# The transposing loads of x, from the fifth on, are issued from ScalarE's queue

## The chip, the cores and the metric

The kernel runs on one core of one Trainium2 chip. Its time is the device time of one execution in microseconds (us). The runs compared are several executions of each kernel; one more execution of each was recorded by the hardware profiler, and the tables below come from that one.

The core has five engines that work side by side, each with its own in-order instruction stream: TensorE (PE in the profile; its weight loads are PEld), VectorE (DVE), ScalarE (ACT), GpSimd (POOL) and SyncE (SP), which here does nothing but issue DMAs. A DMA is issued by an instruction in an engine's stream and then carried out by the core's 16 DMA engines; a semaphore tells of its landing. In the profile "SPq" and "ACTq" are the instructions that an engine's sequencer handles by itself, DMA issues among them.

## The reference

One ConvNeXt-V2 block on an image of 512 x 512 pixels with 96 channels, in bfloat16:

```python
out = jnp.zeros_like(x)
for i in range(K):                       # K = 3: depthwise 3x3, taps dw
    for j in range(K):
        out = out + xp[:, i:i+H, j:j+W, :] * dw[i, j]
h = _layernorm(out, axis=-1)             # over the 96 channels
h = jnp.einsum('bhwc,ce->bhwe', h, w1)   # 96 -> 384
h = _gelu(h)
gx = jnp.sqrt((h * h).sum(axis=(1, 2), keepdims=True) + 1e-6)
nx = gx / (gx.mean(axis=-1, keepdims=True) + 1e-6)
h = grn_gamma * (h * nx) + grn_beta + h
h = jnp.einsum('bhwe,ec->bhwc', h, w2)   # 384 -> 96
return x + h
```

The sum of squares gx runs over all pixels, so the second matrix product can't begin before all blocks have passed the first.

## The kernel before

The image is cut into 128 blocks of four rows. The program has two stages. In the first, every block is loaded, convolved, normalised and put through the first product and the GELU, only to gather gx (and to keep some of the results). In the second, the hidden values are recomputed or read back, and the second product, the sum with x and the store follow. The change touches the first stage alone.

The first stage is written as a loop over slots s, and each slot holds a piece of work for several blocks at different depths of the pipeline. In the order in which slot s records them:

- `load_x(s + 4)` (L214, called at L785): a transposing DMA that brings block s + 4 of x, channels on partitions, into one of six places of the ring `xT`.
- `stage_read` (L606): one DMA that reads a normalised block back from DRAM, `ynT<-yn_dram`. It waits for the four writes of that block, made one slot earlier.
- `stage_write` (L601): four DMAs `yn_dram<-yn` that write the block which GpSimd normalised in the slot before.
- `stage_bcast` and `stage_rows` (L585, L567), each in one slot of four: four DMAs `rbc<-r_dram` and two DMAs `r_dram<-rt` that carry the row of 1/sqrt(variance) of a batch of four blocks through DRAM and spread it over the partitions.
- `store_next` (L706): a third of a finished block of GELU outputs, `g_dram<-g`, in most slots.
- On GpSimd: `stage_newton`, `stage_norm` (`yn<-y_bf,rbc`), the squares `ysq<-y_bf`, and `stage_rstd`.
- On TensorE, ScalarE and VectorE, interleaved by `mlp_units` (L658): the nine taps of the convolution of block s in three bursts, and the units of the first product of a block read two slots earlier. ScalarE runs ten activations in such a slot: units 0, 2, 3, 4, 6 and 7, the evacuation `y_bf` of the convolution, and units 8, 10 and 11. VectorE takes the statistics of the GELU outputs and one third of the evacuation (`CAST y_bf`), before which stands the turn of `stage_turn` (L561), once in four slots.

All the DMAs of this list are issued by SP, in this order; there are 128 blocks, and every engine's stream keeps the order of the program (`InOrder`, L24 to L40, fixes it, which is why most instructions carry L35 as their line). In the first slots, before the product has blocks to work on, ScalarE also makes the squares.

The framework gives each DMA that SP or ScalarE issues one of eight semaphores, in turn. A DMA that is given a semaphore waits until the DMA that held it before has landed. The turn runs over the DMAs of both engines, in the order of the framework's own schedule.

Of the kernel before, what the change touches and what calls it, by code (L numbers as in the profile page):

```python
# [56 lines left out]
def kernel(  # L57
# [125 lines left out]
    with ExitStack() as p1:  # L183
        pe, dve, act, pool, sp = (InOrder(tc, e) for e in (nc.tensor, nc.vector, nc.scalar, nc.gpsimd, nc.sync))
# [28 lines left out]

        def load_x(b):  # L214
            s0 = b % NXT * GR
            sp.dma_start_transpose(
                out=xt_all[:, :, s0:s0 + GR, :].rearrange("p k r w -> p k (r w)"),
                in_=bass.AP(x.tensor, x.offset + b * GR * W * C, [[4 * C, GR * W4], [1, 4 * C]]))

# [5 lines left out]
        for b in range(min(2, NBLK)):  # L225
            load_x(b)
        act.activation(out=warm[:], in_=warm[:], func=ACTF.Gelu_apprx_tanh)
        for b in range(2, min(4, NBLK)):
            load_x(b)
# [552 lines left out]
        for s in range(last_slot + 1):  # L782
            get = lambda kind: at.get((s, kind), [])
            if s + 4 < NBLK:
                load_x(s + 4)  # L785
# [53 lines left out]
            else:  # L839
                b = mlp[0]  # L840
# [163 lines left out]
```

## Time and profile before

| what | before |
| --- | --- |
| time, three runs | 1546.52 us median (1536.55 to 1554.59) |
| profiled execution | 1546.16 us, of which the recorded span is 1544.4 us |
| busy, of the span | PE 1428.2 us (92%), ACT 1372.3 (89%), POOL 1297.4 (84%), DVE 1096.2 (71%) |
| transposing loads | 128, all issued by SP, the first at 0.7 us, the last at 915.1 us |
| first stage, convolution | TensorE's matmuls on `xT` start at 7.9 us and go on to 950 us |
| second stage | from about 1040 us to the end, some 500 us; no load of this kind in it |
| DMA | 427.57 MB; SP's queue 319.76 MB, GpSimd's 103.43 MB, ScalarE's 0.15 MB |

Busy time does not count DMA issues: SP has no busy time at all, and what its stream does is seen in the timeline alone. A line of the timeline gives the start in us, the length in us, the engine, the line, the operation, output<-input and how many instructions were merged; in brackets the idle time of the engine before it and what ended it. In the view of a tile the three numbers behind a group are the shortest, the median and the longest duration in ns.

### The profile page before, as it was taken

The numbers are of one execution on the slowest core, as the hardware profiler recorded it, in microseconds if no ns is written. First come the engines' busy times: TensorE is split into PE (matmuls) and PEld (weight loads), VectorE is DVE, ScalarE is ACT, GpSimd is POOL, SyncE is SP. The second block draws the span as 40 slices with busy tenths as digits, with TensorE's granted clock in tenths as the row PEclk, the third lists the DMA queues.
The fourth block names the chain that finished last, engine by engine and source line by source line (L and its number), as shares of the span: only waits on it lengthen the run. The fifth ranks groups of instructions, "written<-read, shape, count | busy, mean of one in ns | idle before, by whom it ended". The sixth has DMA issues, their size and how long they took to land. (4 is left out here: it accounts for less than half of the span.)

```text
span 1544.4 us, 66344 instructions
## 1 busy us (share of the span) xinstructions
PE 1428.2 (92%) x29245; PEld 879.6 (57%) x29245; DVE 1096.2 (71%) x1997; ACT 1372.3 (89%) x1588; POOL 1297.4 (84%) x917
## 2 busy tenths in 40 slices
PE   7879989989999899999999989879999999998998
PEld 3435545545454454555455545447777767776776
DVE  4617868888887888888888888885555555554555
ACT  5759988979898898998898979999999999999997
POOL 2558897898789889988898889729999999999997
PEclk9989999999999999999999999999999999999999
DMA  8878999999999999999999997659999999999997
GB/s 148 178 171 204 238 203 240 237 238 225 241 233 237 232 234 239 257 225 247 234 243 235 241 233 214 194 178 358 396 365 379 418 412 414 412 412 405 409 415 281
DMA packets 349994, 427.57 MB, mean 277 GB/s; under 512 B 230122, under 2 KB 279882, under 8 KB 345226
## 3 DMA queue, kind: packets, MB, share of 16 engines
q1 hardware_dynamic: 333464, 319.76, 78.3%
q0 software_dynamic: 14880, 103.43, 16.8%
q8 instruction: 229, 3.75, 1.0%
q14 instruction: 59, 0.48, 0.1%
q10 hardware_dynamic: 1362, 0.15, 0.1%
HBM read 216.68 MB, written 156.22 MB: 241 GB/s over the span
## 5 line engine op out<-in xcount | busy, mean ns | idle before, releaser
L35 ACT ACTIVATE g<-PS 128x512 bf16<-128x512 f32 (+2 forms) x1062 | 731.7, 799 | 101.1 <-PE PS L35 47.2
L35 DVE BATCH_NORM_STATS2 bst<-g 128x6 f32<-128x512 bf16 x1110 | 680.1, 677 | 135.3 <-ACT g L35 133.9
L35 PE MATMUL PS<-ynT,w1p 128*128 128x512 bf16 x2181 | 612.3, 384 | 26.8 <-ACT g L35 7.9
L35 ACT ACTIVATE gr<-PS 128x1536 bf16<-128x1536 f32 x360 | 498.9, 1458 | 19.3 <-PE PS L35 15.0
L35 POOL TENSOR_TENSOR yn<-y_bf,rbc 128x1536 bf16<-128x1536 bf16 x126 | 389.8, 3096 | 146.9 <-DMA rbc<-r_dram 79.1
L35 DVE TENSOR_TENSOR o_sb<-PS,xb 128x384 bf16<-128x384 f32 x512 | 277.2, 556 | 228.0 <-PE PS L35 182.4
L35 PE MATMUL PS<-xT,Wd 32*32 32x512 bf16 (+2 forms) x15336 | 382.4, 367 | 58.7 <-DVE y_bf L35 35.8
L299 POOL TENSOR_TENSOR xb<-xr,B2c 128x1536 f32<-128x1536 bf16 x118 | 368.2, 3132 | 5.1 <-DVE o_sb L35 2.8
L35 PEld LDWEIGHTS <-Wd 32*32 32x32 bf16 x15336 | 180.8, 89 | 268.4 <-issue 220.6
L35 POOL TENSOR_TENSOR ysq<-y_bf 128x1536 bf16<-128x1536 bf16 x114 | 313.4, 2749 | 11.4 <-DVE y_bf L35 11.4
L35 PEld LDWEIGHTS <-w1p 128*128 128x128 bf16 x2181 | 172.2, 98 | 176.6 <-issue 91.6
L35 PEld LDWEIGHTS <-gr 128*128 128x128 bf16 x4296 | 212.2, 98 | 71.8 <-issue 15.4
L35 PE MATMUL PS<-W2s,gr 128*128 128x96 bf16 x4224 | 223.8, 206 | 10.3 <-DVE o_sb L35 9.9
L35 ACT ACTIVATE y_bf<-PS 128x1024 bf16<-128x1024 f32 (+1 forms) x135 | 139.9, 1041 | 37.2 <-PE PS L35 37.2
L35 PEld LDWEIGHTS <-g 128*128 128x128 bf16 x1704 | 104.9, 98 | 60.8 <-issue 28.0
L35 PE MATMUL PS<-w1p,ynT 128*128 128x256 bf16 (+2 forms) x822 | 125.2, 272 | 8.8 <-ACT xT L35 3.2
L35 PE MATMUL PS<-g 128*128 128x128 bf16 x1464 | 122.4, 220 | 1.3 <-DVE PS L35 1.3
L35 DVE CAST y_bf<-PS 128x512 bf16<-128x512 f32 x121 | 81.0, 670 | 36.9 <-PE PS L35 36.8
L35 PEld LDWEIGHTS <-gl 128*128 128x128 bf16 x1680 | 82.9, 98 | 24.9 <-issue 3.0
L35 PE MATMUL PS<-W2s,gl 128*128 128x96 bf16 x1680 | 89.7, 206 | 1.4 <-DVE o_sb L35 1.1
L35 PEld LDWEIGHTS <-ynT 128*128 128x128 bf16 x822 | 63.9, 97 | 31.2 <-issue 13.4
L254 POOL DMA_DIRECT2D xr<-in_x_dram x115 | 63.8, 555 | 14.2 <-POOL xb L299 14.2
(99 smaller groups left out, 566.6 us busy)
## 6 DMA issues: line engine op xcount, KB each, us to landing
g_dram<-g SPq DMA_DIRECT2D x105, 512.0 KB
gl<-g_dram POOLq DMA_DIRECT2D x35, 1536.0 KB, 11.2
yn_dram<-yn SPq DMA_DIRECT2D x512, 96.0 KB
ynT<-yn_dram SPq DMA_DIRECT2D x128, 384.0 KB
out_dram<-o_sb SPq DMA_DIRECT2D x127, 384.0 KB
xr<-in_x_dram POOLq DMA_DIRECT2D x123, 384.0 KB, 7.0
ynT<-yn_dram SPq DMA_DIRECT2D x85, 512.0 KB
rbc<-r_dram SPq DMA_DIRECT2D x124, 128.0 KB
```

The costliest lines, as they stand in the source:

```text
L35: r = f(*a, **k)
L254: pq.dma_start(out=xr[:], in_=x[0, r0:r0 + GR].rearrange("r w c -> (r w) c").rearrange("(p g) c -> p g c", g=PXP))
L299: pq.tensor_tensor(out=xb[:], in0=grp[q]["xr"][:], in1=bias[:, None, :].to_broadcast([128, PXP, C]), op=ALU.add)
```

## The change

The issue of the load goes to ScalarE's stream for blocks 4 to 127; blocks 0 to 3, which are loaded ahead of the loop, stay with SP. The call stays where it was: `load_x(s + 4)` is the first thing that slot s records. The descriptors, the places in the ring and the data are the same.

```diff
         def load_x(b):
             s0 = b % NXT * GR
-            sp.dma_start_transpose(
+            (sp if b < 4 else act).dma_start_transpose(
                 out=xt_all[:, :, s0:s0 + GR, :].rearrange("p k r w -> p k (r w)"),
                 in_=bass.AP(x.tensor, x.offset + b * GR * W * C, [[4 * C, GR * W4], [1, 4 * C]]))
```

In the built program the streams of PE and DVE are the same as before, instruction by instruction. ScalarE's stream gains 124 DMA issues, each ahead of the first activation of its slot; SP's loses them. The waits follow: since ScalarE's stream has by then passed activations that wait for the convolution of the slot before, its load needs no wait for TensorE any more, but it keeps a wait for the DMA that held its semaphore before. In the steady slots that is nearly always the first or the second of the four writes `yn_dram<-yn` of the same slot, which SP issues; in a few slots it is a read or ScalarE's own load of the slot before. The first load on ScalarE, block 4, also waits for the landings of blocks 2 and 3, which SP issues.

## The prediction

> **What bounds the kernel now.** I read the busy times by stage first, then the timeline of SP's stream, then ScalarE's. Nothing of this kind is issued after 915.1 us, so the stage to read is the steady part from 200 to 915 us:
>
> ```profile
> core 0: us, PE busy (x) PEld busy (x) DVE busy (x) ACT busy (x) POOL busy (x), PEclk, DMA share, GB/s
> 200.00:915.00 715.00, 661.10 (x15915) 361.71 (x15914) 596.01 (x1026) 627.78 (x931) 619.23 (x463) 0.98 1.02 236
> ```
>
> PE is busy 92%, ACT 88%, POOL 87%: no engine is full, and each is near it. SP is missing from this table. Its stream over two slots:
>
> ```profile
> 500.05 0.32 SPq L35 DMA_DIRECT2D ynT<-yn_dram  x1
> 500.50 3.13 SPq L35 DMA_DIRECT2D yn_dram<-yn  x4
> 503.68 1.18 SPq L35 DMA_DIRECT2D r_dram<-rt  x2
> 504.96 0.41 SPq L35 DMA_DIRECT2D g_dram<-g  x1
> 505.47 1.93 SPq L35 DMA_TRANSPOSE xT<-in_x_dram  x1
> 507.58 0.45 SPq L35 DMA_DIRECT2D ynT<-yn_dram  x1
> 508.09 2.77 SPq L35 DMA_DIRECT2D yn_dram<-yn  x4
> 510.90 2.45 SPq L35 DMA_DIRECT2D rbc<-r_dram  x4
> 513.44 0.37 SPq L35 DMA_DIRECT2D g_dram<-g  x1
> ```
>
> Each issue starts about 0.05 to 0.2 us after the one before has ended. Adding up the single records from 200 to 915 us, SP is issuing for 625 of 715 us (writes 263, loads of x 191, rbc 60, reads 44, stores 40, r_dram 26); 38 of the other 90 us stand between a load and the read behind it, which often waits for its writes to land. So SP waits for hardly anything of the engines: its stream is full. Loads follow each other every 7.63 us, 30.5 us for four. ScalarE shows what is undisturbed:
>
> ```profile
> 234.86 3.90 ACT L35 ACTIVATE g<-PS 128x1024 bf16<-128x1024 f32 x6 [0.25 <-PE PS L35]
> 238.59 1.08 ACT L35 ACTIVATE y_bf<-PS 128x1024 bf16<-128x1024 f32 x1
> 239.50 2.07 ACT L35 ACTIVATE g<-PS 128x1024 bf16<-128x1024 f32 x3
> 241.92 1.51 ACT L35 ACTIVATE g<-PS 128x1024 bf16<-128x1024 f32 x2 [0.35 <-ACT g L35]
> ```
>
> From 234.86 to 241.92 a slot takes 7.06 us with 0.35 us idle. The difference between 7.06 and 7.63 are longer gaps. They come through GpSimd, which waits for the broadcast that SP issues late in its slot; GpSimd's view of the normalisation says so (idle us, times):
>
> ```profile
>   DMA rbc<-r_dram: 42.0, 14
>   ACT g L35: 29.0, 9
> ```
>
> Late GpSimd makes the turn on VectorE late, then the cast of y_bf, then TensorE's next burst.
>
> **What SP gains.** Without the load, SP's slot is a read (0.47), four writes (2.82), the gaps (0.25) and, before the next read, the landing of the fourth write, which by the semaphore updates in the trace comes 3.0 us after its issue ends: 6.6 us, with broadcast, rows and store inside that landing. That is less than ScalarE's 7.06, so SP stops being the bound. Late next is ScalarE: 4 x 7.06 = 28.2 us for four slots, and 0.6 for the aggregates on VectorE (2.77 us about every eleventh block, of which some 1.6 reach ScalarE). Against 30.5 that is 1.7 us, and with the loads from 116 to 915 us there are 26 such groups: **-44 us**.
>
> The Trainium skill (DMA: Bandwidth & Descriptors, section "Issuing engines are not separate DMA queues") says that issuing from several engines saves only the sequencer's time, usually small beside the DMA. Here the row speaks against "small": 2.06 us of the 6.0 that a load takes from issue to landing, on a stream that is full. By the page the gain would be near nothing, and a sum by it 44 us higher than the one below.
>
> **What ScalarE pays: the issue.** On SP the issue took this long, in the first slots and in the steady ones:
>
> ```profile
> L35 SPq DMA_TRANSPOSE xT<-in_x_dram x8: 1350/1451/2276, 65.4 to 108.9; - x8
> L35 SPq DMA_TRANSPOSE xT<-in_x_dram x93: 1388/2064/3113, 205.4 to 908.7; - x93
> ```
>
> The longer ones mostly stand right behind a store of g (mean 2.11 us, 81 of 93). ScalarE's stream has no such store, but the stage and its traffic are those of the second row. I take 2.06 and keep 1.45 as the lower end. Its cover is ScalarE's lead: the sequencer hands over activations ahead of their execution. Where its record of the wait ahead of a slot's first activation is seen, it begins about 1.85 us (median; 1.7 to 2.2 for most) before that activation starts, while unit 8 still runs and 10 and 11 are handed over. An issue fits in there, and only the rest delays the slot: with the 93 measured durations against the leads of the 104 slots, 25 us in all at 2.06 (most slots +0.3), 3 us at 1.45. One slot in four I count in the loop below: **+19**.
>
> **What ScalarE pays: the wait.** Its load of slot s now waits, in most slots, for the second write of the same slot to land. TensorE's and VectorE's work of the slot is queued behind it through unit 0 and the evacuation. Today the first write begins 0.9 to 3.0 us after the slot's first activation (mean by place in the batch), and the second lands 5.2 us after that; it would have to land some 1.8 us ahead of it. So SP and GpSimd must come to stand about 9 us earlier against ScalarE than now, which ScalarE pays once, by waiting: **+9**. From then on a loop closes that was open: cast of y_bf ends 5.3 us into slot t; squares on GpSimd 2.75; rstd 1.55; newton 2.95; norm 3.1; two writes 1.4; landing 3.8; issue 2.06; handover 0.1: 23.0 us to the first activation of slot t+3, where 3 x 7.06 = 21.2 stand now. Newton and rstd come once in four slots, so 1.8 us for each of 26 groups: **+47** (+32 with an issue of 1.45; nothing, if SP and GpSimd find slack that I do not see, for in the other slots the same loop is 18.5). SP's own waits for loads that hold its semaphores are an issue and 3.9 us of landing, a slot or more earlier; I cost them at nothing, under SP's new slack of 0.5 us a slot.
>
> **The start.**
>
> ```profile
> 0.74 21.00 SPq L35 DMA_TRANSPOSE xT<-in_x_dram  x8
> 10.60 1.02 ACT L35 ACTIVATE y_bf<-PS 128x1024 bf16<-128x1024 f32 x1 [7.71 <-PE PS L35]
> ```
>
> Block 3 is issued until 8.1 us and lands 3.2 later, at 11.3; only then may ScalarE issue block 4 (1.5 to 2), and the evacuation at 10.60 is behind it: **+3**. In the other early slots ScalarE idles 1.4 to 2.8 us ahead of an evacuation, which hides the issue; each load is needed three slots later, so a late one costs nothing.
>
> The skill (same page, section "Silent corruption: two transposing streams in flight at once") asks that the later stream's first transpose wait for the earlier stream's landing. This is that wait. No run here shows what happens without it; by the page it is due, and by the row it costs 3 us once.
>
> **Sum.** -44 + 19 + 9 + 47 + 3 = +34 us on the profiled execution's own 1546.16 us (span 1544.4 and 1.8 around it), which is 0.4 us under the median of the runs: **1580 us**, +2.2%. The second stage, from 1040 us, is untouched.
>
> **The rivals.**
>
> - *SP's freed stream wins* (faster). If SP and GpSimd run a slot ahead by themselves, the wait is over when ScalarE comes to it, and the issue takes 1.45: -44 + 3 + 3 = -38, **1508**. For it: SP's new slot of 6.6 us is shorter than 7.06, and SP alone holds the rate today. Against: GpSimd has 27 to 28 us of work in four slots of 28.2, so it can hardly draw ahead. It decides when the second write lands earlier than 1.85 us before the first activation of its slot.
> - *A draw.* The issue takes 1.45, the loop stays: -44 + 3 + 9 + 32 + 3 = +3, **1549**.
> - *The issue is not covered.* If the semaphore comes late in nearly every slot, the lead is lost and every issue stands whole between two slots: 104 x 2.06 = 214 on top of the 59 us of the start, the shift and the loop, less the 44: at most **1775**; with half of it, about 1665. For it: landings spread by over 1 us (3.0 to 4.6 for the second write), and every spread now hits ScalarE. It decides when the write lands later than 2.06 us before the first activation is due, in slots without newton too.
>
> That the loads stay with SP after all is excluded: they stand in ScalarE's stream of the built program.
>
> **How the numbers follow.** The forecast's case (1562 to 1630) gets 0.43, SP's gain 0.22, the draw 0.17, the uncovered issue 0.18. With the lower edge at 1512, a little above the rival's 1508, and the upper at 1665 about 2 in 10 are left out, half on either side. About 1% (15 us) is what a measurement of this kernel can tell from no change. Faster by more: 0.23; within: 0.17; slower: 0.60.
>
> **What would show it.** Right: SP's stream with gaps in the steady part; the second write of a slot landing close to the time ScalarE's sequencer reaches the load; ScalarE's gaps at slot starts grown to 0.6 us, and to 2 us or so in the newton slots; GpSimd's 42 us for rbc smaller. Wrong: issues on ScalarE of 1.4 us and gaps of 0.3, at 7.06 us a slot (SP's gain), or gaps of 2 us in every slot (no cover). Wrong as well, if issues on both queues slow each other down, which no row of this trace shows, as no two issues of its steady part run side by side on SP and ScalarE.

## The result, and the profile after

| what | before | after |
| --- | --- | --- |
| time, median of four runs each | 1546.43 us (1536.55 to 1554.59) | 1657.83 us (1640.01 to 1682.66) |
| profiled execution | 1546.16 us, span 1544.4 | 1640.01 us, span 1638.2 |
| last load of x is issued at | 915.1 us | 1008.6 us |
| from there to the end | 629.3 us | 629.6 us |
| mean from load to load, block 20 to block 127 (107 slots) | 7.61 us | 8.44 us |

The ratio of the times is 1.0639, with a 95% interval of 1.0521 to 1.0757 (two slower executions of the changed kernel, 1666.20 and 1682.66 us, at a lower clock, are left out of it though not of the median, so that 1546.43 x 1.0639 = 1645 us is the time to compare). The change made the kernel slower. The second stage is as long as before; at the start 4.8 us are lost up to the load of block 20 (105.7 us against 100.9); the rest, 107 x 0.83 = 89 us, is lost in the steady part of the first stage.

The busy times by stage of the changed kernel, for the same window as before:

```profile
core 0: us, PE busy (x) PEld busy (x) DVE busy (x) ACT busy (x) POOL busy (x), PEclk, DMA share, GB/s
200.00:915.00 715.00, 611.44 (x14253) 326.07 (x14253) 528.47 (x910) 559.01 (x828) 554.54 (x418) 0.96 0.92 211
```

Every engine does 8 to 11% less work in the same 715 us, and the DMA engines move 211 GB/s instead of 236: no engine has become the bound. The timeline of SP's stream:

```profile
506.31 1.17 SPq L35 DMA_DIRECT2D r_dram<-rt  x2
507.59 0.52 SPq L35 DMA_DIRECT2D g_dram<-g  x1
508.30 0.31 SPq L35 DMA_DIRECT2D ynT<-yn_dram  x1
508.67 3.32 SPq L35 DMA_DIRECT2D yn_dram<-yn  x4
512.03 2.63 SPq L35 DMA_DIRECT2D rbc<-r_dram  x4
514.76 0.37 SPq L35 DMA_DIRECT2D g_dram<-g  x1
515.30 0.40 SPq L35 DMA_DIRECT2D ynT<-yn_dram  x1
515.75 4.04 SPq L35 DMA_DIRECT2D yn_dram<-yn  x4
519.89 0.53 SPq L35 DMA_DIRECT2D g_dram<-g  x1
530.90 0.31 SPq L35 DMA_DIRECT2D ynT<-yn_dram  x1
```

SP has gaps now. From 200 to 1000 us it issues for 416 of 800 us, and 184 us of the rest stand between a store and the read behind it (mean 2.2 us). What SP waits for, by the view of its own waits in the 715 us (us in total, times, longest):

```profile
SPq L35 <- DMA yn_dram<-yn: 178.5, 101, 10.2
SPq L35 <- DVE y_bf L35: 61.3, 20, 7.0
SPq L35 <- DMA ynT<-yn_dram: 34.7, 23, 4.2
```

The first row was, before,

```profile
SPq L35 <- DMA yn_dram<-yn: 23.3, 36, 2.4
```

so SP now stands waiting for its own writes to land. ScalarE's timeline beside it:

```profile
506.60 1.53 ACTq L35 DMA_TRANSPOSE xT<-in_x_dram  x1
506.96 1.17 ACT L35 ACTIVATE g<-PS 128x512 bf16<-128x512 f32 x2
508.56 3.90 ACT L35 ACTIVATE g<-PS 128x1024 bf16<-128x1024 f32 x6 [0.43 <-PE PS L35]
512.29 1.09 ACT L35 ACTIVATE y_bf<-PS 128x1024 bf16<-128x1024 f32 x1
513.20 1.59 ACT L35 ACTIVATE g<-PS 128x1024 bf16<-128x1024 f32 x2
514.42 2.66 ACTq L35 DMA_TRANSPOSE xT<-in_x_dram  x1
514.58 0.70 ACT L35 ACTIVATE g<-PS 128x512 bf16<-128x512 f32 x1
517.20 3.90 ACT L35 ACTIVATE g<-PS 128x1024 bf16<-128x1024 f32 x6 [1.93 <-PE PS L35]
520.93 1.08 ACT L35 ACTIVATE y_bf<-PS 128x1024 bf16<-128x1024 f32 x1
521.84 2.08 ACT L35 ACTIVATE g<-PS 128x1024 bf16<-128x1024 f32 x3
530.23 1.32 ACTq L35 DMA_TRANSPOSE xT<-in_x_dram  x1
531.75 3.79 ACT L35 ACTIVATE g<-PS 128x1024 bf16<-128x1024 f32 x5 [7.84 <-PE PS L35]
```

At 506.60 the load is issued while activations run, and the slot opens with 0.43 us idle. At 514.42 the issue ends at 517.08 and the slot opens right behind it, after 1.93 us idle. At 530.23 the issue begins right behind the landing of a write (530.21 us), 6.3 us after the last activation has ended, and everything behind it has waited too. The gap ahead of a slot's first activation is 1.67 us in the mean over the 95 loads from 200 us on, against 0.80 before. That difference, 0.87 us, is about the whole loss of a slot (0.83). In 64 of the 95, the first activation starts within 0.25 us of the end of the load's issue. The 95 gaps are 158 us in all. In 42 of these us the load has not been issued yet, 92 lie under its issue, and 25 come after it. This tells where ScalarE idles and not yet why: the issue also hides other delays that end under it.

Why the write was so late at 530 is seen in the landings, which the semaphore updates in the trace give. The load, both stores, the read and the four writes issued from 514 to 520 us all landed 11 to 12.6 us after their issue; that is the worst stretch. From 200 to 900 us, from the end of the issue to the landing in us (10th percentile, median, 90th):

| DMA | before | after |
| --- | --- | --- |
| writes `yn_dram<-yn` | 2.32, 3.61, 4.62 | 2.96, 4.63, 7.29 |
| load of x | 2.69, 3.92, 4.30 | 3.04, 4.91, 7.69 |
| read `ynT<-yn_dram` | 3.78, 4.44, 5.20 | 3.45, 5.50, 8.06 |
| store `g_dram<-g` | 3.04, 3.98, 4.86 | 3.18, 4.48, 7.92 |

All four land later, by 0.5 to 1.1 us in the median and by 2.7 to 3.4 at the 90th percentile. For the writes it matters whether a load of x is in flight, that is, issued and not landed when the write's issue ends. From 200 us to the last load, with none in flight, the median and the 90th percentile are 2.86 and 3.72 us before (78 writes) and 2.53 and 3.73 after (37). With one in flight they are 3.74 and 4.69 before (296) and 4.73 and 7.24 after (343). The DMA engines' own work has not grown: the part of the page on DMA queues shows (packets, MB, share of 16 engines), before and then after,

```profile
q1 hardware_dynamic: 333464, 319.76, 78.3%
q10 hardware_dynamic: 1362, 0.15, 0.1%
```

```profile
q1 hardware_dynamic: 139032, 270.98, 52.1%
q10 hardware_dynamic: 195794, 48.93, 21.3%
```

That is 78.4% of 1544.4 us and 73.4% of 1638.2, or 1211 us and 1202. The packets take the same time in the sum, and still the DMAs land later.

### The profile page after: what moved, and what is told of

Read it like the earlier page. It is cut to its first block, busy times and chain, and to the rows that moved or that the text cites. A ratio compares the mean times of both kernels' runs of the same rounds, so it can differ in the third digit from the quotient of the medians.

```text
span 1638.2 us, 66328 instructions
## 1 busy us (share of the span) xinstructions
PE 1458.0 (89%) x29245; PEld 885.6 (54%) x29245; DVE 1095.7 (67%) x1997; ACT 1374.3 (84%) x1588; POOL 1299.0 (79%) x917
## 5 line engine op out<-in xcount | busy, mean ns | idle before, releaser
L35 PE MATMUL PS<-ynT,w1p 128*128 128x512 bf16 x2181 | 627.8, 387 | 93.4 <-ACT g L35 69.0
L35 PE MATMUL PS<-xT,Wd 32*32 32x512 bf16 (+2 forms) x15336 | 390.3, 373 | 49.0 <-issue 32.8
L35 PE MATMUL PS<-g 128*128 128x128 bf16 x1464 | 126.5, 224 | 1.3 <-DVE PS L35 1.3
```

Source lines behind the costliest of these rows:

```text
L35: r = f(*a, **k)
```

## The experiments

The changed kernel gave three candidates. **Wait**: ScalarE's load waits for SP's write of the same slot, and so closes the loop that the prediction feared. (Of the 95 loads, 51 wait for the second write of their slot, 18 for the first and 14 for the third, the others for other DMAs.) **Issue**: the time in which ScalarE's sequencer issues the load isn't covered. **Queues**: loads and the other DMAs are in flight on two queues, and all land late. Under the last it was open whether it takes full DMA engines, any second queue, or a transposing load on one of the two. Us per slot means the mean from the load of block 20 to the last, in the one profiled execution. Ratios are of several executions against the kernel before, with their 95% interval.

**1. The semaphores dealt anew** (changed kernel). Each DMA that SP issues first in a slot is listed behind ScalarE's load, so that the load takes its semaphore from a DMA of an earlier slot. Nothing else changes in the streams.

```diff
...
             if hasattr(r, "ins"):
                 self._tc.keep_in_program_order(r)
+                if name == "dma_start" and self._eng is self._tc.nc.sync and LAST_X:
+                    self._tc.add_manual_dep(r.ins, LAST_X.pop(), ...)   # order in the list, no semaphore
...
-            (sp if b < 4 else act).dma_start_transpose(
+            r = (sp if b < 4 else act).dma_start_transpose(
...
+            if b >= 4:
+                LAST_X[:] = [r.ins.name]
```

> Every engine's stream is that of the changed kernel, instruction by instruction; only the framework's list is told that SP's first DMA of a slot stands behind ScalarE's load of that slot. So the eight semaphores are dealt differently: the load of slot s waits for a DMA of slot s-1 or s-2 and no longer for a write of slot s. Theory 'wait' (ScalarE stalls because its load waits for the landing of a write that SP issues in the same slot): the waits ahead of the load, 120 us in sum from 200 us on, mostly go, and with SP's stream freed the time falls to the old kernel's or below, 1500 to 1550 us. Theory 'queues' (loads and other DMAs from two queues in flight at once slow each other's landing, whatever ScalarE waits for): the median landing of a write stays at 4.6 us and the time stays over 1600 us. Theory 'issue' (ScalarE can't cover the issue itself): 1570 to 1600 us, with gaps of 1 us or more at most slot starts and no wait ahead of the load.

Measured: 1622.91 us, 1.0456 (1.0406 to 1.0505), 8.35 us per slot (the profiled execution is the slowest of the four, 1638.48 us). ScalarE idled 6 us ahead of its issues instead of 42, and 58 us under them instead of 92, but the writes landed as late as in the changed kernel (2.75, 4.69, 6.64). (The expectation counts the sequencer's own wait, part of which passes while activations still run.) With most of the wait gone, 1.8 of the 6.4% come back; the two intervals leave room for 0.5 to 3.1. The late landings stay.

**2. A small DMA on ScalarE** (kernel before, x on SP). ScalarE issues a copy of 1.7 KB at the place where the changed kernel has the load.

```diff
+        tinyt = consts.tile([9, C], bf16, name="tinyt")
...
             if s + 4 < NBLK:
+                act.dma_start(out=tinyt[:], in_=dw.rearrange("kh kw c -> (kh kw) c"))
                 load_x(s + 4)
```

> The loads of x are all back on SP; ScalarE issues in their place, once in each slot, a load of 1.7 KB into a scratch tile that nothing reads (0.6 us of issue in the trace of the old kernel). It takes a semaphore in the turn, and waits for one, a write of the slot before. Theory 'wait': within 1% of the old kernel, 1535 to 1565 us, since the wait is a slot older than in the changed kernel. Theory 'queues': the same, for next to nothing is moved by the second queue. Theory 'issue': 0.6 us fits under the lead of 1.85 us, 1546 us as well. If it is over 1575 us, a DMA on ScalarE costs something that none of the three has.

Measured: 1559.88 us, 1.0056 (1.0033 to 1.0079), 7.65 us per slot. The view of its tile (shortest, median, longest in ns) shows the issue:

```profile
L35 ACTq DMA_DIRECT2D tinyt<-in_dw_dram x93: 278/279/302, 203.3 to 913.9; - x93
```

A wait and a short issue on ScalarE cost 0.04 us per slot in the profiled execution, the fastest of eight, and 0.6% by the ratio, while the writes land as before (3.60 in the median). All three candidates had expected this, so it parts none of them; it shows that a DMA on ScalarE as such costs little.

**3. The writes ahead of the read** (changed kernel). SP's writes no longer stand behind a read that waits for landings, so that they leave and land earlier for ScalarE.

```diff
-            for b in get("read"):
-                stage_read(b)
             for b in get("write"):
                 stage_write(b)
+            for b in get("read"):
+                stage_read(b)
```

> The changed kernel with SP's writes of a slot recorded ahead of its read, so that the writes no longer stand behind a read that waits for the landing of the writes of the slot before (184 us between a store and the read behind it, from 200 to 1000 us). The load still waits for a write of its own slot. Theory 'wait': the writes are issued 2 to 4 us earlier against ScalarE, and the waits ahead of the load fall by half or more: 1540 to 1590 us. Theory 'queues': the landing stays long, and the time stays within 2% of the changed kernel's, 1620 to 1680 us. Theory 'issue': the same, 1620 to 1680.

Measured: 1651.18 us, 1.0653 (1.0615 to 1.0691), 8.43 us per slot: no gain. The median landing of a write fell to 4.04 us and ScalarE's idle time ahead of the issues to 29 us, but the late landings stayed (90th percentile 7.09).

**4. The four writes as one DMA** (kernel before). To learn what SP's full stream is worth.

```diff
-            for r in range(GR):
-                sp.dma_start(out=yn_dst(b, r), in_=yn[32 * r:32 * r + 32, :, :])
+            t = yn_dram[b]
+            sp.dma_start(out=bass.AP(t.tensor, t.offset, [[W, GR], [NI * GR * W, 32], [GR * W, NI], [1, W]]),
+                         in_=yn[:])
```

> The old kernel (loads on SP), with the four writes of a block issued as one DMA of the same 384 KB. It measures the other reading of the old kernel by itself: if SP's full stream bounds the steady part (625 of 715 us issuing), and one issue of 384 KB costs about half of the four (2.8 us), SP gains some 1.4 us a slot and the steady part falls from 7.63 to 7.1 us a slot, 1490 to 1510 us in all. If SP's stream isn't the bound, 1535 to 1555 us.

Measured: 1825.68 us, 1.1779 (1.1725 to 1.1833), 9.60 us per slot. The writes' issue fell from 263 to 40 us of the 715, yet SP was issuing for 641 us, because its other issues grew: the load of x, 2064 ns in the median before, now

```profile
L35 SPq DMA_TRANSPOSE xT<-in_x_dram x75: 1754/3656/6582, 203.3 to 914.5; - x75
```

So the length of an issue on SP is not fixed: it grew beside a slower DMA of the same stream. The time of this kernel says nothing of a shorter stream, since the single DMA itself landed 8.4 us after its issue in the median. The next run repeats the question with another layout.

**5. The four writes as one DMA of 128 x 3 KB** (kernel before). The DRAM copy keeps the tile's order; the reads gather 1 KB runs instead.

```diff
-    yn_dram = dram.tile([NBLK, C, GR * W], bf16, name="yn_dram")
+    yn_dram = dram.tile([NBLK, GR * C, W], bf16, name="yn_dram")
...
     def yn_src(q):
-        return yn_dram[q].rearrange("c (r w) -> c r w", r=GR)
+        return yn_dram[q].rearrange("(r c i) w -> (c i) r w", r=GR, i=NI)
...
-            for r in range(GR):
-                sp.dma_start(out=yn_dst(b, r), in_=yn[32 * r:32 * r + 32, :, :])
+            sp.dma_start(out=yn_dram[b].rearrange("(p i) w -> p i w", i=NI), in_=yn[:])
...                                               # the second stage's reads take yn_src as well
```

> The kernel before (x on SP), with the four writes of yn as one DMA of 128 x 3 KB into a DRAM layout that keeps the tile's order, and the read gathering four 1 KB runs for each channel instead of one of 4 KB. SP has three issues fewer in each slot; bytes and the sum of 1 KB and larger packets stay. Theory SP (its stream of issues is the bound, the reading of the prediction): the writes' 2.8 us of issue a slot become about 0.7, SP's slot 5.5 us, so slots of 7.06 to 7.2 us, ratio 0.965 to 0.975. Theory DMA (the 16 engines are full, packets in flight for 709 of 715 us, and long issues are back-pressure): the loop does not get shorter, ratio 0.99 to 1.01, and the other issues on SP take longer than before.

Measured: 1588.19 us, 1.0253 (1.0214 to 1.0292). Of the 46 us that its profiled span is longer, 33 lie in the second stage, where the reads are in 1 KB runs; in the first stage a slot takes 7.71 us against 7.61. The window and what SP waited for in it:

```profile
200.00:915.00 715.00, 654.75 (x15943) 359.56 (x15915) 589.46 (x1015) 624.38 (x925) 618.70 (x463) 0.98 0.95 235
```

```profile
SPq L35 <- PE PS L35: 399.4, 93, 8.0
```

SP issues for only 375 of the 700 us from 200 to 900, and waits most of the rest for TensorE to leave the place in the ring. (The view counts into the issues. By the records, 286 us without an issue stand ahead of loads, and 91 of the 93 loads start right behind an update of TensorE's semaphore.) An SP with half its time free brings no shorter slot. One thing speaks against taking this as the whole answer: other DMAs landed later in this run, the write at 5.02 us and the broadcast at 5.10 in the median, where it was 3.60 and 2.84. So theory SP, on which the prediction's largest gain rested, is not borne out: freeing the stream is not enough. What a free SP with unchanged landings would bring is not shown.

**6 and 7. Ordinary copies in place of the transposing loads, on SP and on ScalarE.** The same bytes in 384 packets of 1 KB instead of 1536 of 256 B. The transposition is left out, so the convolution works on channels in the wrong places. The two differ only in the queue, and the second has the same waits ahead of the load as the changed kernel.

```diff
-            sp.dma_start_transpose(
-                out=xt_all[:, :, s0:s0 + GR, :].rearrange("p k r w -> p k (r w)"),
-                in_=bass.AP(x.tensor, x.offset + b * GR * W * C, [[4 * C, GR * W4], [1, 4 * C]]))
+            ...                                   # b < 4: as before
+                sp.dma_start(                     # 7: act.dma_start
+                    out=xt_all[:, :, s0:s0 + GR, :],
+                    in_=bass.AP(x.tensor, x.offset + b * GR * W * C, [[12 * 128, 128], [512, NI], [128, GR], [1, W4]]))
```

> The kernel before, with the loads of x from the fifth on as ordinary copies of the same number of bytes (384 packets of 1 KB in place of 1536 of 256 B): no transposition, so the channels are wrong and the output with them. Theory DMA: a load takes about 1.3 us of all engines instead of 2.7 (the price of 384 1 KB packets of the writes), the share of DMA falls from 1.02 to about 0.85, and the slots go to ScalarE's 7.06 to 7.2 us: ratio 0.965 to 0.975. Theory SP: the issue of a load falls to that of a write (0.7 us) and the ratio is the same, but then issues of the other DMAs keep their lengths (writes 0.7 us); by theory DMA they get shorter too. If neither bounds, 0.99 to 1.01.

> The changed kernel with the same ordinary copies in place of the transposing loads, on ScalarE's queue (output wrong in the same way). Against the same copies on SP. If a second queue as such makes all landings late, or ScalarE's wait for SP's writes: 3 to 6% slower than the copies on SP, landing of a write 4.5 us. If it takes full DMA engines, or the 1536 small packets of the transposing load mixed with others: within 1% of the copies on SP, landing of a write near 3.6 us or under it.

Measured, on SP: 1521.54 us, 0.9823 (0.9771 to 0.9875), 7.34 us per slot. On ScalarE: 1543.24 us, 0.9959 (0.9935 to 0.9982), 7.57 us per slot. The windows, on SP and on ScalarE:

```profile
200.00:915.00 715.00, 679.66 (x16633) 375.56 (x16631) 614.68 (x1064) 649.55 (x965) 643.69 (x482) 0.99 0.81 245
```

```profile
200.00:915.00 715.00, 664.21 (x16168) 365.31 (x16145) 598.24 (x1035) 631.65 (x940) 627.29 (x475) 1.00 0.79 240
```

Landing of a write: 2.54, 3.73, 4.98 on SP; 1.86, 3.66, 5.17 on ScalarE. The move costs 0.22 us per slot here, 1.4% (1543.24 / 1521.54), where it costs 0.83 with transposing loads, and the writes land no later. The other DMAs do, but less than in the changed kernel: load, read and store by 0.4 to 0.7 us in the median (0.5 to 1.1 there), and by at most 0.8 at the 90th percentile (2.7 to 3.4 there). Neither the second queue as such nor the wait and loop bring the writes' late landings or the long tails. But two things differ from the changed kernel: the load itself (no transposition, a quarter of the packets) and the DMA share, 0.8 for 0.9. The base speaks only half for full DMA engines: with a fifth of their time freed it gained 0.27 us per slot, not the 0.4 to 0.5 expected. ScalarE's issue is also shorter here, 547 ns; 25 us of idle time lie under the issues, and 21 ahead of them.

**8. The stores on ScalarE's queue** (kernel before, x on SP): another second queue, with 128 packets of 4 KB in most slots.

```diff
-                sp.dma_start(out=g_dram[whole.index(b)][:, h * n:h * n + n],
+                act.dma_start(out=g_dram[whole.index(b)][:, h * n:h * n + n],
```

> The kernel before (x on SP), with the stores g_dram<-g of the first stage issued on ScalarE's queue at their old place in the program's order. A second queue with 128 packets of 4 KB at a time. If a second queue as such lets packets of two DMAs mix and all land late: landing of a write from 3.6 to 4 us or more, ratio 1.02 to 1.06. If only the mixing of the transposing loads does it: landing of a write 3.6 us or under, ratio 0.99 to 1.01 (ScalarE's own issue was worth 0.6% in the run with a small DMA). Theory SP: its stream is relieved of 40 us of issues, ratio 0.97 to 0.99.

Measured: 1568.68 us, 1.0129 (1.0065 to 1.0192), 7.64 us per slot in the profiled execution, the fastest of the four. Landing of a write 2.28, 3.83, 4.94: a little later. This lies between the two sides: a second queue costs something even with transposing loads left on SP, but not 6%. SP's stream, relieved of the stores, brings no gain here either.

**9 and 10. Both kernels with quartered stores.** They take away DMA load and leave the transposing loads as they are. A quarter of each store of g is made, and the second stage reads it four times; the hidden values of the stored blocks are wrong in both.

```diff
...                                               # g_dram smaller; the second stage reads it four times
+                m = 512
-                sp.dma_start(out=g_dram[whole.index(b)][:, h * n:h * n + n],
-                             in_=flat(b)[:, h * n:h * n + n])
+                sp.dma_start(out=g_dram[whole.index(b)][:, h * m:h * m + m],
+                             in_=flat(b)[:, h * n:h * n + m])
```

> The kernel before (x on SP) with a quarter of each store g_dram<-g of the first stage: 128 x 1 KB in place of 128 x 4 KB. The second stage reads that quarter four times over, so bytes read there stay and the output is wrong for the stored blocks. It is the base of the next run; a store's three quarters are some 1.5 us of all 16 DMA engines, at 0.78 stores a slot. If the DMA engines' time bounds the old loop, its loads come every 7.1 to 7.3 us instead of 7.61 (mean from the 20th load to the last), ratio 0.965 to 0.98; if not, 7.5 to 7.65 and 0.99 to 1.0.

> The changed kernel with the same quartered stores. To be set against the run before it, as 8.44 us a slot of the changed kernel stands against 7.61 (+0.83). Theory full engines (two queues hurt because the engines have no slack, and small loads are drained alongside the writes): with slack the difference falls to +0.3 or less, 2% of the time, landing of a write near 3.7 us. Theory transposition (a transposing load beside ordinary DMAs of another queue is slow by itself, whatever the load): the difference stays +0.6 to +0.85 us a slot, 4.5 to 6.5%, landing of a write 4.3 us or more. ScalarE's wait for the write is there in both (one write later in the turn for many slots, as the scheduler deals the semaphores anew).

Measured: 1532.89 us, 0.9888 (0.9859 to 0.9916), 7.45 us per slot with x on SP; 1631.46 us, 1.0523 (1.0464 to 1.0582), 8.38 us per slot with x on ScalarE. The windows, in that order:

```profile
200.00:915.00 715.00, 670.47 (x16266) 369.87 (x16265) 607.82 (x1048) 639.27 (x951) 631.88 (x479) 0.98 0.85 193
```

```profile
200.00:915.00 715.00, 627.35 (x14722) 338.84 (x14723) 544.86 (x939) 577.17 (x854) 574.55 (x425) 0.96 0.82 175
```

The base's 7.45 us lies between its two sides again. The move costs 0.92 us per slot, 6.4% (1631.46 / 1532.89), no less than with full stores, at a DMA share close to that of runs 6 and 7. The writes land at 1.91, 3.22, 4.23 us with x on SP and at 2.73, 4.30, 7.37 with x on ScalarE. So the late landings don't need DMA engines as full as in the kernel before. In these runs they come when the transposing loads, with their 1536 packets, go out on another queue than the writes and reads.

**11. The writes ahead of the read in the kernel before**, the edit of run 3; a try at a faster kernel.

> The kernel before with the four writes recorded ahead of the read in each slot. A version to beat both: the writes leave SP 0.5 us earlier and the read that waits for its block's writes stands behind new issues, so the 38 us of SP's gaps between a load and a read go. Theory SP (its stream is the bound): 38 us over the loop, ratio 0.975 to 0.98. Theory DMA engines: 0.99 to 1.01.

Measured: 1603.69 us, 1.0346 (1.0316 to 1.0376), 8.02 us per slot, against both theories. The writes land sooner (median 3.08), but the broadcast, now right behind the read, lands at 4.20 us instead of 2.84, the load's issue grows to 2.58 us in the mean, and GpSimd's wait for the broadcast from 42.0 to 61.0 us. The order in SP's one queue is worth 3% by itself. No run here is a faster kernel that computes the block.

**12. The ordinary copies on ScalarE, dealt as in run 1.** Transposition left out as in run 7.

```diff
-                act.dma_start(
+                r = act.dma_start(
...
+                LAST_X[:] = [r.ins.name]
```

> The ordinary copies on ScalarE's queue (384 packets of 1 KB, output wrong as before), with the semaphores dealt so that a load takes its place in the turn ahead of the reads and writes of its slot: it then waits for a DMA of an earlier slot, as in the run with dealt transposing loads (8.35 us a slot against 8.44). Copies on SP took 7.34 us a slot, on ScalarE 7.57. If the wait for SP's write of the same slot is what the 0.22 us are, 7.3 to 7.4 us a slot, ratio 0.98 to 0.985. If it is the issue on ScalarE or the second queue, 7.5 to 7.6, ratio 0.99 to 1.0.

Measured: 1541.44 us, 0.9942 (0.9904 to 0.9981), 7.50 us per slot, where 7.3 to 7.4 or 7.5 to 7.6 were the two sides. The time is that of run 7 within the intervals; the profiled executions differ by 0.07 of the 0.22 us. ScalarE idles neither ahead of the issues nor under them here (0 us each), so most of what is lost without transposition is neither the wait nor the issue. The writes land a little later than in run 7, at 3.99 us in the median.

## Why the prediction held, and where it was wrong

The sign was right and the time lies in the range, but the loss was 94 us in the profiled execution where 34 was the forecast. The 1645 us of the ratio are nearer to the half-covered case of the third rival, 1665, than to the forecast. That the range held is in part luck, since the one gain in the sum did not come at all: without the -44 the same sum is +78. By its steps:

- **SP's stream is the bound; -44.** Not borne out, and the step that failed first: SP got its gaps, and the slot got longer. (The four terms of SP's new slot add up to 6.5 us and not 6.6, which changes nothing.) SP's time was full of issues whose length is not fixed. The load's issue, 2.06 us on SP, takes 1.54 in the median on ScalarE:

```profile
L35 ACTq DMA_TRANSPOSE xT<-in_x_dram x84: 1321/1544/2664, 199.7 to 910.1; - x84
```

  In run 4 the same issue on SP was 3.66 us; in run 5 SP had half its time free, and the slot took 7.71 us. What did shorten the old slot was less work for the DMA engines (runs 6 and 9: -0.27 and -0.16 us), though SP issued less there too (506 and 609 of 715 us, for 625), so that these runs don't part the two. What holds the rest above ScalarE's 7.06 us is not settled; run 11 shows that the order in SP's queue counts.
- **The issue; +19 at 2.06 us, 3 at 1.45.** Its length came out near the lower end, but the cover did not hold. The lead that was to hide it is spent where the wait ahead of the load is long: 64 of 95 slots begin with the end of the issue, and ScalarE idles 92 us under the issues, where 19 were counted. This is the rival's mechanism. Its own reason, spreads of 3.0 to 4.6 us in the landings, was not enough: with writes that land as before the move costs 0.22 us (run 7, with a shorter issue).
- **The loop; +47 and the shift +9.** The form was right: ScalarE waits ahead of its load for SP's writes and idles 42 us over 95 loads for it, and TensorE, VectorE and SP hang behind it. The term that was mis-sized is the landing, taken as 3.8 us from the old trace. It became 4.6 in the median and over 7 in every tenth write. Neither the shift nor the newton slots show by themselves: the gap was to be 0.6 us in most slots and 2 us in one of four, 0.95 in the mean, and is 1.67. Breaking the loop (run 1) brings back 0.09 us per slot of 0.83 in the profiled execution, and 1.8 of the 6.4% in the ratios.
- **The start; +3.** Right in kind and about in size: 4.8 us are lost up to the load of block 20. Block 4 is issued 2.6 us later than before (10.75 us against 8.14), behind the landing of block 3, and the evacuation waits behind it:

```profile
10.75 1.50 ACTq L35 DMA_TRANSPOSE xT<-in_x_dram  x1
12.30 1.02 ACT L35 ACTIVATE y_bf<-PS 128x1024 bf16<-128x1024 f32 x1 [9.39 <-PE PS L35]
```

- **The signs to look for.** SP's gaps came as said, and GpSimd's wait for the broadcast is smaller, 35.5 us against 42.0, though hardly so per slot (0.42 against 0.45), and it buys nothing. What would make the prediction wrong was named as issues on both queues slowing each other. The issues did not get longer; the landings came later.

The Trainium skill (DMA: Bandwidth & Descriptors, "Issuing engines are not separate DMA queues") says that DMAs of all issuing engines run on the same 16 DMA engines and interleave, and that a second issuer saves sequencer time alone. The prediction weighed its second half, and used the 2.06 us against it. The first half was the one to weigh: the later landings, 3.61 us before and 4.63 after, fit such an interleaving, though no run shows it packet by packet. The page's section does not tell kinds of DMA apart; runs 7 and 10 do, with 0.22 against 0.92 us per slot.

What is shown: the move costs 6.4% with transposing loads, under either load of the DMA engines, and 1.4% with ordinary copies. The writes land 1.0 to 1.1 us later in the first case and 0 to 0.3 in the second (medians), and in the first it is those that are issued while a load is in flight. The wait (run 1) and a second queue by itself (runs 7, 8 and 12) are the smaller part. What stays open is why a transposing load and ordinary DMAs on two queues land later together, and whether it is the transposition or the number of small packets, which no run separates. Packets cost the same in the sum. Also open is how the 0.6 to 0.7 us beyond the case of ordinary copies divide between late landings and an issue that is 1 us longer. The 92 us of idle time under the issues, against 25 in run 7, say that the issue may well be a large part, but no run lengthened the issue without transposing.

## What to carry to other kernels

A queue whose issues fill its time need not be the bound: look whether its issue times stretch, and free it in a side experiment before counting its time as a gain. Before a transposing load is moved to another engine's queue than the DMAs it runs beside, measure how the landings of all of them change, and price every wait on a landing with the new spread, not with that of the old trace. A lead that hides an issue is spent when the issue itself has to wait first.

## What the runs showed of the hardware

- One load of x is 1536 packets of 256 B. In the kernel before, 90% of the loads have begun their last packet within 5.73 us of the issue's start; on ScalarE's queue within 8.02, though the first packet starts earlier (1.40 us against 2.07 in the median).
- An issue's length on SP changes with what else SP issues: the load took 2.06 us in the mean there in the kernel before, 1.60 in run 5 and 4.02 in run 4. On ScalarE's queue, the ordinary copies took 547 ns nearly every time.
- A long wait can cost twice, through TensorE's clock. The stretch after the 7.8 us gap, by windows of 5 us (the column before the last two is the granted clock):

```profile
520.00:525.00 5.00, 4.92 (x163) 3.09 (x143) 4.59 (x10) 3.92 (x7) 4.67 (x2) 1.00 1.16 162
525.00:530.00 5.00, 0.17 (x2) 0.00 (x0) 0.00 (x0) 0.00 (x0) 4.09 (x14) 0.91 0.73 208
530.00:535.00 5.00, 3.35 (x21) 1.30 (x20) 2.19 (x4) 3.08 (x5) 2.95 (x1) 0.50 0.88 88
535.00:540.00 5.00, 4.86 (x125) 2.73 (x124) 4.05 (x7) 3.95 (x6) 2.26 (x1) 0.91 0.89 262
```

  TensorE idles from 525 to 530 us, and runs the next 5 us at half its clock. From 105 us to the last load it ran at half clock for 31 us before and 79 after (27 and 92 in runs 9 and 10). Half of the added 49 us, 24 of the 89, is an estimate of the most that this can have cost. The Trainium skill (TensorE: Matmul & The Clock Gate, section "HAM oscillation — how this bites in real kernels") describes this for a wait on a DMA between tiles; the rows agree.
